# Storing two batches' last 64 tokens by one transfer, and the second batch's late Z behind the first relu, in the finish of an attention and spectral-mix kernel

## The chip, the cores and the metric

The kernel runs on one core of one Trainium2 chip. The metric is the time of one execution on the device, in microseconds (us). Engines are named as the profile names them: PE is TensorE (PEld its weight loads), DVE is VectorE, ACT is ScalarE, POOL is GpSimd, SP is SyncE, which issues all loads and stores here.

## The reference

Eight batches of 576 tokens go through attention with 8 heads of 64 and then through a spectral mix over the tokens. Cut to what matters:

```python
# attention: causal window of 128, a bias that falls with distance, softmax, then attn @ v
x = attn_out.transpose(0, 2, 1, 3).reshape(B, S, H * D)      # 8 x 576 x 512
X = np.fft.rfft(x, axis=1)[:, :64]                            # 64 modes of each batch
Yr = Xr @ w_r - Xi @ w_i ; Yi = Xr @ w_i + Xi @ w_r           # a 512 x 512 pair per mode
y = np.fft.irfft(Y, n=S, axis=1)
u = x + y
out = u + np.maximum(u @ w_ch, 0.0)                           # 8 x 576 x 512, float32
```

The two weight tensors of the modes are 64 x 512 x 512 float32 each and are read once: most of the traffic.

## The kernel before

**Stages.** Attention runs over pairs of heads and batches, its results stay in SBUF as `x_sb` and `x4`. The mode weights stream in through a ring (`_load_w`), and each mode's matmuls (`_modes`) follow. While the last weights stream in, the products `x @ w_ch` are made for all tiles (`_xw`, kept as `hl`). After the last weight comes `_finish` (L753 to L809), and only there does the output leave the core.

**Tiles.** The output is written in 36 tiles of 128 rows by 512 columns, listed in `g.seq` (L88 to L92). A batch has 576 = 4 x 128 + 64 tokens. So a pair of batches gives four full tiles of the first, four of the second, and one tile, `x4`, whose upper 64 rows are the last 64 tokens of the first batch and whose lower 64 rows are those of the second. The tiles are numbered 0 to 35; the mixed ones are 8, 17, 26 and 35.

**The finish.** The spectrum of a batch (`Z`, and `ZW = Z @ w_ch`) is complete for the first modes early. The last modes' part, the late Z, comes from `_z_late` (L710) into PSUM for four batches at a time, and `_z_take` (L730) copies one batch's 32 partitions of it to SBUF: `ZW` on ACT, `Z` on DVE, or on ACT for every fourth batch. Then the loop of L776 walks over the tiles:

- at step i PE makes tile i: `mm` is the argument of the relu and `y` the inverse transform, both in PSUM (`_known`, and the two `_pair` calls);
- then, at fixed steps, `_z_late` for batches 4 to 7 (L785) and `_z_take` for the batch whose first tile is three tiles ahead (L787);
- then tile i - 1 gets its nonlinearity. Tiles with way "a" take a relu on ACT (L794); tiles with way "q" take a copy of `y` on ACT (L797) and a maximum on DVE (L798). Tiles 0, 1 and the last five are "a", and two of each five between;
- then tile i - 2 gets its sum `o`, on DVE for "a" (L803) and on POOL for "q" (L806). `o` has 12 buffers (L801); `mm` and `y` have three PSUM buffers each, and a new tile takes the one that was freed first;
- `store` (L769) is called right behind the sum for "a", one step later for "q".

The order of the work on each engine is the order of these lines: it is written by hand, nothing moves it afterwards. SP takes the stores one after the other; each has one of eight completion semaphores in turn, so a store is issued only when the one eight before it has landed.

**The stores.** A tile that lies in one batch is stored as one transfer of 256 KB (L772). A mixed tile is stored as two transfers of 64 rows, 128 KB each (L774), since its halves lie 576 x 512 elements apart in the output.

Of the kernel before, what the change touches and what calls it, by code (L numbers as in the profile page):

```python
# [16 lines left out]
P = 128  # L17
# [16 lines left out]
def kernel(  # L34
# [60 lines left out]
    with tc.manual_schedule(engines={ET.SP, ET.PE, ET.Activation, ET.DVE, ET.Pool}):  # L95
        with ExitStack() as wctx:
# [116 lines left out]
            for m0, mg in todo:  # L213
                _modes(g, last, m0, mg, last=True)
                if NM - 4 <= m0 < NM - 1:
                    _idle(g, BUSY)
            mctx.close()
        _finish(g)


# [443 lines left out]
def _pair(nc, out, lhsT, rhs, **kw):  # L664

    for h in range(2):
        nc.tensor.matmul(  # L667
            out[64 * h : 64 * h + 64], lhsT=lhsT[h], rhs=rhs[h], tile_position=(0, 64 * h), **kw)
# [41 lines left out]
def _z_late(g, b0, psum):  # L710

    nc = g.nc
    zwp = psum.tile([P, g.DM], FP32, tag="zwp", name="zwl")
    zp = psum.tile([P, 4, P], FP32, tag="zp", name="zl")
    for et in range(4):
        for c in range(4):
            l = g.ZT[:, et, 3].rearrange("p a m b -> p (a m) b")[:, :, b0 + c]
            nc.tensor.matmul(
                zwp[32 * c : 32 * c + 32], lhsT=l, rhs=g.wch[:, et],
                start=(et == 0), stop=(et == 3), tile_position=(0, 32 * c))  # L720
    for et in range(4):
        for c in range(4):
            l = g.ZT[:, et, 3].rearrange("p a m b -> p (a m) b")[:, :, b0 + c]
            nc.tensor.matmul(
                zp[32 * c : 32 * c + 32, et], lhsT=l, rhs=g.ident_b, start=True, stop=True,
                tile_position=(0, 32 * c))
    g.late = (zp.rearrange("p a b -> p (a b)"), zwp)


def _z_take(g, b):  # L730
    nc = g.nc
    zp, zwp = g.late
    ks = slice(32 * (b % 4), 32 * (b % 4) + 32)
    nc.scalar.copy(g.ZW[ks, b], zwp[ks])
    if b % 4 == 2:
        nc.scalar.copy(g.Z[ks, b], zp[ks])
    else:
        nc.vector.tensor_copy(g.Z[ks, b], zp[ks])


def _known(g, i):

    nc = g.nc
    x = g.seq[i][0]
    g.mm[i] = g.fps.tile([P, g.DM], FP32, tag="mm", name="mm")
    g.y[i] = g.fps.tile([P, g.DM], FP32, tag="y", name="y")
    _pair(nc, g.mm[i], [g.ident2] * 2, [g.hl[:, i, h] for h in range(2)], start=True, stop=False)
    if g.way[i] == "a":
        _pair(nc, g.y[i], [g.ident_b[:, 0:64], g.ident_b[:, 64:128]], [x] * 2,
              start=True, stop=False)  # L750


def _finish(g):  # L753

    nc, tc = g.nc, g.tc
    N = len(g.seq)
    with ExitStack() as fctx:
        pool = fctx.enter_context(tc.tile_pool(name="fin", bufs=4))  # L760
        lps = fctx.enter_context(
            tc.tile_pool(name="lps", bufs=1, space=bass.MemoryType.PSUM, side="right"))
        first = [min(i for i, t in enumerate(g.seq) if t[1][0][0] == b and t[1][1][0] == b)
                 for b in range(g.B)]
        _z_late(g, 0, lps)
        _z_take(g, 0)
        o, r, y = {}, {}, {}

        def store(i):  # L769
            for h, (b, s) in enumerate(g.seq[i][1]):  # L770
                if h == 0 and g.seq[i][1][1] == (b, s + 64):
                    nc.sync.dma_start(out=g.out[b, s : s + P, :], in_=o[i])  # L772
                    break
                nc.sync.dma_start(out=g.out[b, s : s + 64, :], in_=o[i][64 * h : 64 * h + 64])  # L774

        for i in range(N + 3):  # L776
            if i < N:
                if i >= 3:
                    _known(g, i)
                ft = [g.FT[:, b % 4, s : s + 64] for b, s in g.seq[i][1]]  # L780
                _pair(nc, g.mm[i], ft, [g.ZW[:, b] for b, _ in g.seq[i][1]],
                      start=False, stop=True)
                _pair(nc, g.y[i], ft, [g.Z[:, b] for b, _ in g.seq[i][1]],
                      start=(g.way[i] == "q"), stop=True)
            if i == first[3] - 1:  # L785
                _z_late(g, 4, lps)
            for b in range(1, g.B):  # L787
                if i == first[b] - 3:
                    _z_take(g, b)
            j = i - 1  # L790
            if 0 <= j < N:
                r[j] = pool.tile([P, g.DM], FP32, tag="r", name="r")
                if g.way[j] == "a":
                    nc.scalar.activation(r[j], g.mm[j], AF.Relu)  # L794
                else:
                    y[j] = pool.tile([P, g.DM], FP32, tag="y", name="ys")
                    nc.scalar.copy(y[j], g.y[j])  # L797
                    nc.vector.tensor_tensor(out=r[j], in0=g.mm[j], in1=g.seq[j][0], op=ALU.max)  # L798
            j = i - 2
            if 0 <= j < N:  # L800
                o[j] = pool.tile([P, g.DM], FP32, tag="o", bufs=12, name="o")  # L801
                if g.way[j] == "a":
                    nc.vector.tensor_tensor(out=o[j], in0=g.y[j], in1=r[j], op=ALU.add)  # L803
                    store(j)
                else:
                    nc.gpsimd.tensor_tensor(out=o[j], in0=r[j], in1=y[j], op=ALU.add)  # L806
            j = i - 3
            if 0 <= j < N and g.way[j] == "q":
                store(j)  # L809
# [30 lines left out]
```

## Time and profile before

| What | Value |
|---|---|
| median of 3 runs | 446.2 us (445.45 to 446.92) |
| the profiled execution | 446.81 us, its span 445.0 us |
| busy share of the span: PE, DVE, ACT, POOL | 74%, 49%, 47%, 23% |
| DMA in the chain that ended last | 50% of the span |
| HBM read, written | 163.58 MB, 9.44 MB |
| stores of 256 KB | 32, median 3.0 us from issue to landing |
| stores of 128 KB | 8, median 2.7 us from issue to landing |
| last mode's sum on DVE ends, first store issued | 408.2 us, 412.0 us |

The span runs from the first to the last instruction of the profiled execution; the rest of its time lies outside. Line numbers are those of the kernel. In a row of the timeline the columns are the start, the length of the merged run, the engine, the line, the operation with its output and input, the shape and how many instructions were merged; the bracket names the idle time ahead of it and what ended it. "SPq" rows are DMA issues: their length is the issue on SP, not the transfer.

### The profile page before, as it was taken

Reading aid. Unit: us, or ns where it says so; the run is one execution under the profiler, and the core shown is the slowest. Engines: PE = TensorE matmul, PEld = TensorE weight load, DVE = VectorE, ACT = ScalarE, POOL = GpSimd, SP = SyncE. Lnnn points to the kernel's source line nnn. Section 1 sums busy time; section 2 is a strip of 40 time slices with the busy share of each in tenths; the row PEclk is TensorE's granted clock in tenths of the full one; section 3 lists DMA queues with packets and bytes.
Section 4 is the critical chain, followed back from the end, with each engine's and each line's share of the span. In section 5 each row is a group of like instructions: output and inputs, shape, how many; then the busy total and the mean of one; then the engine's idle time right before and its main releaser. Section 6 shows DMA issues by size and latency. Waiting matters only on the chain.

```text
span 445.0 us, 11009 instructions
## 1 busy us (share of the span) xinstructions
PE 327.6 (74%) x4626; PEld 217.1 (49%) x4654; DVE 219.2 (49%) x396; ACT 207.1 (47%) x313; POOL 101.6 (23%) x151
## 2 busy tenths in 40 slices
PE   2778889889979977467764656656665488869995
PEld 1445666666757654334443333333333355535553
DVE  6467867788758733242232323333233334512885
ACT  4799968999979501121322212212122132311884
POOL 8644535555533102000000000000000000000883
PEclk9999988999989855685566556566556669969999
DMA  8999989999999999999999999999999999992688
GB/s 294 395 389 385 404 321 399 392 404 405 406 406 402 406 409 404 417 423 425 422 423 425 419 415 418 426 423 423 424 423 423 425 410 417 416 422 122 252 313 288
DMA packets 55217, 173.73 MB, mean 390 GB/s; under 512 B 4992, under 2 KB 4992, under 8 KB 55168
## 3 DMA queue, kind: packets, MB, share of 16 engines
q1 hardware_dynamic: 55168, 173.04, 97.7%
q8 instruction: 36, 0.59, 0.5%
q14 instruction: 13, 0.11, 0.1%
HBM read 163.58 MB, written 9.44 MB: 389 GB/s over the span
## 4 chain that ended last, share of the span: by engine, by line
DMA 50%; PE 26%; ACT 12%; DVE 8%; issue 3%; SPq 1%; POOL 0%; ACTq 0%; POOLq 0%
DMA wi<-in_moe_w_i_dram 50%; PE acc L634 7%; ACT att L437 5%; ACT T L382 4%; DVE att L445 3%; PE mm L667 2%; PE idle L612 2%; PE tqk L372 2%; PE sc L431 2%; PE y L667 2%; PE xw L680 2%; PE av L462 1%; PE av L401 1%; DVE x_sb L480 1%; PE tp L658 1%
## 5 line engine op out<-in xcount | busy, mean ns | idle before, releaser
L684 ACT CAST hl<-xw 64x512 bf16<-64x512 f32 x72 | 41.8, 580 | 163.6 <-PE xw L680 126.1
L634 PEld LDWEIGHTS <-wi 128*128 128x128 bf16 x1024 | 65.7, 105 | 73.6 <-DMA wi<-in_moe_w_i_dram 71.7
L685 DVE TENSOR_TENSOR hl<-xw,hl 64x512 bf16<-64x512 f32 x72 | 49.6, 689 | 85.5 <-ACT hl L684 85.4
L634 PE MATMUL acc<-Xlast,wi 128*128 128x16 bf16 x768 | 55.9, 194 | 48.6 <-DMA wi<-in_moe_w_i_dram 48.5
L634 PEld LDWEIGHTS <-wr 128*128 128x128 bf16 x1024 | 70.7, 106 | 37.2 <-DMA wr<-in_moe_w_r_dram 26.4
L806 POOL TENSOR_TENSOR o<-r,ys 128x512 f32<-128x512 f32 x18 | 22.5, 1279 | 243.7 <-DVE r L798 242.3
L634 PE MATMUL acc<-Xlast,wr 128*128 128x16 bf16 x768 | 63.2, 194 | 19.4 <-DMA wr<-in_moe_w_r_dram 13.5
L445 DVE TENSOR_TENSOR att<-att,mask 128x1024 bf16<-128x1024 bf16 x64 | 55.9, 873 | 36.9 <-ACT att L437 36.6
L437 ACT ACTIVATE att<-sc 128x1024 bf16<-128x1024 f32 x64 | 66.7, 1043 | 9.9 <-PE sc L431 8.7
L382 ACT COPY T<-tqk 128x640 bf16<-128x640 bf16 x92 | 65.6, 767 | 1.7 <-PE tqk L372 1.7
L680 PE MATMUL xw<-wch,xT 128*128 128x512 bf16 x122 | 54.7, 577 | 4.9 <-issue 3.1
L372 PE MATMUL tqk<-ident_b,b 128*128 128x128 bf16 x432 | 39.4, 233 | 10.6 <-POOL b L362 6.4
L660 DVE COPY xT<-tp 128x512 bf16<-128x512 bf16 x36 | 15.2, 423 | 51.8 <-PE tp L658 50.8
L372 PEld LDWEIGHTS <-b 128*128 128x128 bf16 x432 | 27.3, 104 | 22.2 <-issue 11.0
L362 POOL CAST b<-v 128x576 bf16<-128x576 f32 x32 | 27.0, 871 | 17.6 <-issue 8.5
L680 PEld LDWEIGHTS <-xT 128*128 128x128 bf16 x144 | 19.0, 138 | 23.5 <-issue 21.6
L431 PE MATMUL sc<-T,T 64*128 64x256 bf16 (+2 forms) x320 | 26.9, 266 | 1.7 <-ACT att L437 1.0
L362 POOL CAST b<-q 128x576 bf16<-128x576 f32 x32 | 21.5, 699 | 28.9 <-issue 28.9
L362 POOL CAST b<-k 128x576 bf16<-128x576 f32 x32 | 22.0, 714 | 16.3 <-issue 8.5
L462 PE MATMUL av<-vn,att 128*128 128x65 bf16 (+1 forms) x576 | 25.3, 204 | 0.4 <-DVE vn L405 0.2
L462 PEld LDWEIGHTS <-att 128*128 128x128 bf16 (+1 forms) x576 | 21.3, 106 | 3.5 <-issue 0.2
L480 DVE TENSOR_TENSOR x_sb<-av,rec 128x512 bf16<-128x512 f32 x32 | 22.1, 692 | 1.1
(102 smaller groups left out, 437.8 us busy)
## 6 DMA issues: line engine op xcount, KB each, us to landing
wr<-in_moe_w_r_dram SPq DMA_DIRECT2D x85, 768.0 KB, 8.3
wi<-in_moe_w_i_dram SPq DMA_DIRECT2D x85, 768.0 KB, 9.7
q<-in_q_dram SPq DMA_DIRECT2D x32, 288.0 KB, 7.5
k<-in_k_dram SPq DMA_DIRECT2D x32, 288.0 KB, 6.1
v<-in_v_dram SPq DMA_DIRECT2D x32, 288.0 KB, 7.0
out_dram<-o SPq DMA_DIRECT2D x32, 256.0 KB, 3.0
wchf<-in_moe_w_ch_dram SPq DMA_DIRECT2D x4, 256.0 KB, 10.7
out_dram<-o SPq DMA_DIRECT2D x8, 128.0 KB, 2.7
```

Of the source, the lines that this page charges most:

```text
L362: g.nc.gpsimd.tensor_copy(u.b[w][:, :, e], u.raw[w][e])
L372: g.nc.tensor.transpose(u.tp[:, r - r0], u.b[w][:, r].rearrange("p u d -> p (u d)"), g.ident_b)
L382: copy(u.T[w].rearrange("c h (p r) -> c (h p) r", r=g.R)[:, :, r0:r1], u.tp[:, 0 : r1 - r0].rearrange("c r p -> c p r"))
L431: nc.tensor.matmul(sc[:, e, c0 : c0 + nq], lhsT=kT[es, h, _start(kt) : _start(kt) + P], rhs=qT[es, h, kt * P : kt * P + nq], start=True, s ...
L437: nc.scalar.activation(a, sc, AF.Exp, scale=1.0 / math.sqrt(g.D))
L445: nc.vector.tensor_tensor(out=a, in0=a, in1=m, op=ALU.mult)
L462: nc.tensor.matmul(av[o, h, t * (D + 1) : (t + 1) * (D + 1)], lhsT=u.att[min(kt // 2, 1), h][:, f, c0 : c0 + m], rhs=vn[:, g.ST * h + kt, ...
L480: nc.vector.tensor_tensor(out=xo, in0=avv[:, :, 0:4, 0:D], in1=rec[:, :, 0:4].unsqueeze(-1).broadcast_to([P, 2, 4, D]), op=ALU.mult)
L634: nc.tensor.matmul(acc[:, et, :, m - c0, :], lhsT=(wr, wi)[k][:, a].bitcast(BF16)[:, 1::2][:, et * P : (et + 1) * P], rhs=X[:, a, 1 - k : ...
L680: nc.tensor.matmul(xw, lhsT=xT[:, dt], rhs=g.wch[:, dt], start=(dt == 0 and g.way[n] != "q"), stop=(dt == 3))
L684: nc.scalar.copy(g.hl[hi, n, h], xw[hi])
L685: nc.vector.tensor_tensor(out=g.hl[lo, n, h], in0=xw[hi], in1=g.hl[hi, n, h], op=ALU.subtract)
```

## The change

The mixed tiles (8, 17, 26 and 35) are now stored by one transfer each, from 128 partitions of the tile to two blocks of 64 rows in the output. The `_z_take` of the second batch moves in step 1 from ahead of tile 0's relu to behind it; those of the other batches stay where they were.

```diff
         def store(i):
-            for h, (b, s) in enumerate(g.seq[i][1]):
-                if h == 0 and g.seq[i][1][1] == (b, s + 64):
-                    nc.sync.dma_start(out=g.out[b, s : s + P, :], in_=o[i])
-                    break
-                nc.sync.dma_start(out=g.out[b, s : s + 64, :], in_=o[i][64 * h : 64 * h + 64])
+            (b, t), (c, _) = g.seq[i][1]
+            rows = g.out[b, t : t + P, :] if b == c else g.out[b : c + 1, t : t + 64, :]
+            nc.sync.dma_start(out=rows, in_=o[i])
...
-            for b in range(1, g.B):
+            for b in range(2, g.B):
                 if i == first[b] - 3:
                     _z_take(g, b)
             j = i - 1
...
                     nc.vector.tensor_tensor(out=r[j], in0=g.mm[j], in1=g.seq[j][0], op=ALU.max)
+            if i == first[1] - 3:
+                _z_take(g, 1)
             j = i - 2
```

## The prediction

> **What bounds the kernel now.** I read the busy times by stage first. Columns: stretch and its length, PE, PEld, DVE, ACT and POOL busy with instruction counts, TensorE clock, DMA share, GB/s.
>
> ```profile
> 0.00:409.50 409.50, 298.61 (x4352) 200.01 (x4380) 191.97 (x354) 181.56 (x268) 79.04 (x133) 0.77 1.00 401
> 412.00:420.00 8.00, 7.85 (x78) 4.66 (x79) 7.50 (x13) 7.35 (x14) 6.99 (x6) 1.00 0.67 256
> 420.00:440.00 20.00, 19.13 (x190) 11.23 (x182) 17.03 (x27) 15.66 (x29) 15.55 (x13) 1.00 0.85 300
> 440.00:445.00 5.00, 0.00 (x0) 0.00 (x0) 0.69 (x1) 0.11 (x1) 0.00 (x0) 0.99 0.77 288
> ```
>
> Up to 409.5 us the loads fill all DMA engines (share 1.00); the change touches nothing there. In the finish TensorE is busy 98% and 96% of its two long stretches and paces 36 tiles at 0.8 us; the DMA engines have room (0.67, 0.85). The whole change lies in these last 35 us.
>
> The second view is SP's timeline, which holds the stores.
>
> ```profile
> 412.04 7.71 SPq L772 DMA_DIRECT2D out_dram<-o  x9
> 419.84 1.18 SPq L774 DMA_DIRECT2D out_dram<-o  x2
> 421.11 5.53 SPq L772 DMA_DIRECT2D out_dram<-o  x7
> 426.73 1.11 SPq L774 DMA_DIRECT2D out_dram<-o  x2
> 428.46 4.81 SPq L772 DMA_DIRECT2D out_dram<-o  x7
> 434.52 1.11 SPq L774 DMA_DIRECT2D out_dram<-o  x2
> 435.72 5.24 SPq L772 DMA_DIRECT2D out_dram<-o  x9
> 441.05 1.19 SPq L774 DMA_DIRECT2D out_dram<-o  x2
> ```
>
> Four pairs of half stores (L774) stand among 32 full ones; the last pair is the kernel's last work. The chain ends with what releases it:
>
> ```profile
> 439.51 0.61 ACT r L794
> 440.14 0.69 DVE o L803
> ```
>
> DVE ends at 440.83, SP issues at 441.05 and 441.64. The source view of L774 from 440.9 us gives 2.5 to 2.8 us to landing, so the last half lands at 441.64 + 2.5 = 444.14, and 0.86 us close the span of 445.0.
>
> How fast one DMA engine moves a row is in the stretches of half a microsecond at the end, where only stores move:
>
> ```profile
> 440.50:441.00 0.50, 0.00 (x0) 0.00 (x0) 0.34 (x1) 0.00 (x0) 0.00 (x0) 1.00 1.05 406
> 443.00:443.50 0.50, 0.00 (x0) 0.00 (x0) 0.00 (x0) 0.00 (x0) 0.00 (x0) 1.00 1.00 311
> ```
>
> All 16 engines are busy (share 1.0), also at 443, when little but the half stores is left: halves too are dealt to all 16. 406 GB/s over 16 is 25.4 GB/s for one engine, or 0.081 us for a row of 2,048 B. A full store puts 128/16 = 8 rows on each engine (0.65 us), a half 4.
>
> **The relu ahead of the second batch's Z.** Nothing is added; on ACT the second ZW copy and the first relu change places. DVE's order stays, since the first two tiles put no DVE instruction between the two places; PE's and POOL's stay; the step issues no DMA.
>
> ```profile
> 409.49 1.18 ACT L734 CAST ZW<-zwl 32x512 bf16<-32x512 f32 x2 [17.93 <-PE zwl L718]
> 410.69 1.09 ACT L794 ACTIVATE r<-mm 128x512 f32<-128x512 f32 x2
> 411.72 0.59 ACT L797 COPY ys<-y 128x512 f32<-128x512 f32 x1
> 412.50 0.59 ACT L797 COPY ys<-y 128x512 f32<-128x512 f32 x1 [0.20 <-PE y L667]
> 413.15 0.60 ACT L794 ACTIVATE r<-mm 128x512 f32<-128x512 f32 x1
> ```
>
> The first ZW copy ends at 410.07. The relu must wait for tile 0's mm on PE, which the timeline ends at 410.52, so it starts at most 0.17 us sooner than its 410.69, and ACT idles 0.45 to 0.6 us where the copy hid that wait. Behind it queue the copy (0.58), the second relu and tile 2's ys copy: the second relu goes from 411.18 to about 411.8, the ys copy ends near 412.9 instead of 412.31. PE's tile 4 waits for that, as its y takes the PSUM buffer the ys copy frees (starting at 412.49); tile 4's mm then goes from 413.11 to 413.6, and the relu at 413.15 follows. The 0.20 us of slack ahead of the copy at 412.50 is eaten. Against it, tile 0's add ends up to 0.17 sooner, and PE's 0.14 us pause ahead of tile 3's y (412.06 instead of 411.92) may go. Tile 4 itself reads the moved copy at 412.70; it is done by 411.9. I take +0.5 us on everything later, bounds -0.1 to +0.7, and PE has no later slack to absorb it.
>
> **The stores.** 40 issues become 36. A half costs SP 0.56 us (median of L774), but SP waits for its tiles most of the time (DVE's adds alone 13.0 us, its waits from 408 us), so in mid-finish fewer issues are worth 0. In the tail one full store issued at 441.05 with the 3.0 us to landing of the full stores around 440.4 lands at 444.05 instead of 444.14: 0.1 saved.
>
> But the new transfer is of a kind that the trace does not have. In the built program its source is 128 partitions of 2,048 B, its destination 2 x 64 rows with a stride between the two. Every transfer of before has one outermost count, 128 or 64, equal on both sides and a multiple of 16, and is dealt in equal parts of it. This one has 128 on one side and 2 on the other. The bounds are: still 16 parts of 8 rows (the full stores), or one part for each outermost item of the destination, two engines with 64 rows each. I take two parts: equal shares along the outermost count explain every row of the trace, while sixteen would need a cut inside the second dimension, which no transfer here shows. The DMA engines are then no longer interchangeable.
>
> The Trainium skill, page "DMA: Bandwidth & Descriptors", section "Why a DMA increments its semaphore by 16 and not by 1", states that a transfer uses the largest number of engines up to 16 that divides the slowest counts of both sides, and on this queue the lowest-numbered ones; by that the sum is the one below, with the same two engines each time. No run here shows it yet. The same page's "Rules for kernel authors" advises one 128-partition transfer in place of two halves, which speaks for the change and would give the 0.1 us above.
>
> Cost, if the same two engines serve all four merged stores: from the first of them on, each of the pair has 4 x 64 rows plus 8 rows of each of the 7 + 7 + 9 full stores behind, 440 rows, or 440 x 0.0807 = 35.5 us. Spread over 16 it was 216 rows. The window from 419.84 to 441 is 21 us, so the pair runs behind and never dries up: at 426.7 it holds about 5.2 + 4.5 - 5.9 = 3.8 us of work when the next 5.2 arrive. SP then waits for landings (a completion semaphore returns after eight stores), and through the 12 o buffers DVE, POOL and PE wait too; that delays issues, not the pair, which always has several stores queued. Around its rows a store needs 2.0 (fastest full store) - 0.65 = 1.35 us. End: 419.84 + 0.5 + 1.35 + 35.5 + 0.86 = 458.05, against 445.0: **+13.0 us**. The profiled execution took 446.81 with its span of 445.0, so it would take 459.8; the median of the runs, 446.2, lies 0.6 under it, which gives **459.2 us**.
>
> Bounds of this case: a row in 0.077 us, by the page's fastest slice (426 GB/s), -1.6; the relu at -0.1, -0.6; work already queued at the first merged store (halves there land in 3.4 us, the fastest in 2.2), +1.2; two instruction loads on the pair (36 of them take 0.5% of 16 engines' span, 1 us each), +2.0. That is 457.0 to 462.4.
>
> **Rivals.** *Sixteen engines after all*: place, the transfer's split; price, +0.5 from the relu and -0.1 at the last store, 446.6 us, not slower by anything measurable; with its bounds (-0.1 to +0.7; at most one issue of 0.6 saved) 445.5 to 446.8. It decides from about five parts on: the pair stops being the bound when 4 x 128/k + 184 rows fit into the 23 us from 421.2 to 444, some 285 rows, so k above 5. For it: all stores of before use 16. Against: none of them had an outer count below 16.
>
> *Another pair each time*: two engines per merged store, but not the same, so that the backlog drains between. Then only the last one shows: 441.05 + 0.5 + 1.35 + 5.2 + 1.0 queued (3.0 to landing less 2.0) + 0.86 = 450.0, +5.0, 451.2 us. Nothing in the trace tells which engines a narrower transfer gets.
>
> That the stores stay two transfers is excluded: the built program has 36, four of them 2x64x512.
>
> **How the numbers follow.** Same pair 0.82, another pair 0.06, sixteen 0.12. The likeliest gives 459.2. Its own range, 457.0 to 462.4, leaves out the other two cases and the edges of its bounds, so I reach down to the second pair case: 450.5 to 462.5. Faster or slower counts from 0.3% (1.3 us), about what a measurement of this kernel can tell from no change. Both two-engine cases are slower, 0.88; sixteen gives "same" 0.10, and 0.02 for a faster end that its bounds do not reach.
>
> **What would show it.** After the change, the page should list all 36 stores as 256 KB with a longer median to landing, the merged ones 7 us or more; the finish should move about 200 GB/s with a DMA share near 0.5, falling to 2 of 16 engines (0.13) at the end; new waits on landings of out must stand at SP, DVE L803 or POOL L806. The relu step shows as 0.45 us or more idle on ACT at 410.1 and tile 4's y on PE near 413.0. It is wrong if merged stores land in about 3 us, or if the DMA share in the last 5 us is still 0.8.

## The result and the profile after

The changed kernel takes 460.41 us (median of 5 runs, 459.63 to 461.11) against 445.98 us before (5 runs): a ratio of 1.032, 95% interval 1.030 to 1.034, or 14.4 us more. The forecast was 459.2 us, in a range from 450.5 to 462.5. The profiled execution took 459.95 us, with a span of 458.2 us. One of the 23 executions of the kernel before that stand beside the first four experiments took 754.67 us; the ratios leave it out.

The first ZW copy of the finish starts at 408.22 us in this profile and at 409.49 us in the one of before: the weights came in 1.3 us earlier here. So times within the finish are compared from that copy on: 50.0 us to the end of the span, before 35.5 us, which is the whole difference of the medians.

Busy times by stage of the kernel after, columns as in the prediction:

```profile
412.00:420.00 8.00, 7.78 (x92) 4.76 (x88) 6.99 (x11) 6.85 (x13) 7.56 (x7) 1.00 0.69 263
420.00:430.00 10.00, 9.78 (x96) 5.57 (x90) 8.37 (x14) 7.86 (x15) 8.17 (x7) 1.00 0.71 222
430.00:440.00 10.00, 8.63 (x77) 5.03 (x73) 7.30 (x12) 7.11 (x13) 6.66 (x6) 1.00 0.75 246
440.00:453.00 13.00, 0.38 (x4) 0.00 (x0) 1.35 (x2) 0.60 (x1) 0.00 (x0) 0.63 0.51 182
453.00:458.20 5.20, 0.00 (x0) 0.00 (x0) 0.00 (x0) 0.00 (x0) 0.00 (x0) 0.50 0.09 36
```

The engines still work through the tiles at nearly the old pace; the last sum on DVE starts at 440.8, 32.6 us after the first ZW copy, where before it was 30.7. From there on 17 us pass in which only stores move, where before it was 4. The end of that, us by us:

```profile
449.00:450.00 1.00, 0.00 (x0) 0.00 (x0) 0.00 (x0) 0.00 (x0) 0.00 (x0) 0.50 0.13 51
450.00:451.00 1.00, 0.00 (x0) 0.00 (x0) 0.00 (x0) 0.00 (x0) 0.00 (x0) 0.50 0.13 49
...
455.00:456.00 1.00, 0.00 (x0) 0.00 (x0) 0.00 (x0) 0.00 (x0) 0.00 (x0) 0.50 0.14 53
456.00:457.00 1.00, 0.00 (x0) 0.00 (x0) 0.00 (x0) 0.00 (x0) 0.00 (x0) 0.50 0.09 33
```

A DMA share of 0.13 is 2 of 16, steadily for 7 us, and 51 GB/s is two engines at 25.5, one row of 2,048 B in 0.080 us each. That is the pair, alone at work while the other fourteen have nothing left. The completions in the trace say the same of a store that is itself dealt to sixteen: of the full store that SP issued at 446.23 us, fourteen parts landed between 448.06 and 448.21 us, the other two at 451.19 and 451.33. That fits two engines whose older rows come first.

How many engines took part can also be counted on the page. For each part of a transfer on SP's queue the trace has one packet of 4 bytes behind the part's rows; they are the packets "under 512 B", and before there are 4992 of them for 312 transfers, 16 for each. The page of before, then that of after, with its only line for the stores:

```profile
DMA packets 55217, 173.73 MB, mean 390 GB/s; under 512 B 4992, under 2 KB 4992, under 8 KB 55168
```

```profile
DMA packets 55097, 173.73 MB, mean 379 GB/s; under 512 B 4872, under 2 KB 4872, under 8 KB 55048
...
out_dram<-o SPq DMA_DIRECT2D x36, 256.0 KB, 7.0
```

Before, 40 stores with 16 parts each are 640 of these packets. After, 32 stores with 16 and four with 2 are 520. The difference is 120, as the page has it. All 36 stores are of 256 KB, and their median to landing went from 3.0 to 7.0 us.

Who waits now, from SP's and DVE's lists of waits since 408 us (total us, times, longest):

```profile
SPq L835 <- DMA out_dram<-o: 9.1, 1, 9.1
SPq L772 <- DMA out_dram<-o: 5.6, 4, 3.5
```

```profile
DVE o L803 <- DMA out_dram<-o: 1.9, 2, 1.3
```

SP waits for landings before it may issue, DVE for an output buffer, and at the end SP waits 9.1 us for the last store. Before, landings cost SP 1.7 us at the end, and DVE nothing.

The relu step, on ACT and for tile 4's y on PE:

```profile
409.42 0.60 ACT L792 ACTIVATE r<-mm 128x512 f32<-128x512 f32 x1 [0.62 <-PE mm L667]
410.04 0.58 ACT L734 CAST ZW<-zwl 32x512 bf16<-32x512 f32 x1
410.64 0.60 ACT L792 ACTIVATE r<-mm 128x512 f32<-128x512 f32 x1
411.13 1.07 ACT L795 COPY ys<-y 128x512 f32<-128x512 f32 x2
```

```profile
411.76 0.41 PE L667 MATMUL y<-x_sb,ident_b 128*64 128x512 bf16 x2
```

ACT idles 0.62 us ahead of the relu, for PE's mm. Tile 4's y starts 411.76 - 408.22 = 3.54 us after the first ZW copy; before it was 412.49 - 409.49 = 3.00.

### The profile page after: what moved, and what is told of

Same layout as the page of the kernel before. It is cut to its first block, busy times and chain, and to the rows that moved or that the text cites. A ratio compares the mean times of both kernels' runs of the same rounds, so it can differ in the third digit from the quotient of the medians.

```text
span 458.2 us, 11032 instructions
## 1 busy us (share of the span) xinstructions
PE 331.8 (72%) x4654; PEld 215.8 (47%) x4654; DVE 219.3 (48%) x396; ACT 207.0 (45%) x313; POOL 101.1 (22%) x151
## 4 chain that ended last, share of the span: by engine, by line
DMA 46%; PE 25%; ACT 12%; DVE 9%; issue 2%; SPq 1%; POOL 0%; POOLq 0%; DVEq 0%; ACTq 0%
DMA wi<-in_moe_w_i_dram 44%; PE acc L634 6%; ACT att L437 6%; ACT T L382 4%; DVE att L445 3%; PE sc L431 2%; PE tqk L372 2%; PE idle L612 2%; DMA out_dram<-o 2%; PE av L462 2%; DVE x_sb L480 2%; PE xw L680 1%; PE av L401 1%; PE mm L667 1%; PE tp L658 1%
## 5 line engine op out<-in xcount | busy, mean ns | idle before, releaser
L806 POOL TENSOR_TENSOR o<-r,ys 128x512 f32<-128x512 f32 x18 | 22.5, 1274 | 245.8 <-ACT ys L795 243.1
L680 PE MATMUL xw<-wch,xT 128*128 128x512 bf16 x144 | 61.5, 574 | 0.0
L634 PE MATMUL acc<-X,wi 128*128 128x16 bf16 x256 | 18.5, 193 | 5.9 <-DMA wi<-in_moe_w_i_dram 5.9
```

The costliest lines, as they stand in the source:

```text
L634: nc.tensor.matmul(acc[:, et, :, m - c0, :], lhsT=(wr, wi)[k][:, a].bitcast(BF16)[:, 1::2][:, et * P : (et + 1) * P], rhs=X[:, a, 1 - k : ...
L680: nc.tensor.matmul(xw, lhsT=xT[:, dt], rhs=g.wch[:, dt], start=(dt == 0 and g.way[n] != "q"), stop=(dt == 3))
```

## The experiments

Theory A is the forecast's: each merged store is dealt to two DMA engines, always the same, and their queue becomes the bound. Theory B blames the two-block address pattern itself, theory C the moved copy. All kernels keep the order of before for the relu unless said.

| Run | Mixed tiles | Median us, beside before | Ratio, 95% interval |
|---|---|---|---|
| stores only | all merged | 460.43, 446.4 | 1.033 (1.030 to 1.036) |
| relu only | halves | 446.72, 446.4 | 1.0005 (0.999 to 1.002) |
| 62 and 2 rows | each half in two | 461.4, 446.4 | 1.035 (1.033 to 1.038) |
| 48 and 16 rows | each half in two | 446.2, 446.4 | 1.0006 (0.999 to 1.002) |
| last only | one merged | 452.26, 445.84 | 1.014 (1.013 to 1.016) |
| first three | three merged | 456.47, 445.84 | 1.023 (1.022 to 1.025) |
| 57 and 7 rows | each half in two | 452.52, 445.84 | 1.015 (1.014 to 1.017) |
| POOL's queue | all merged | 458.32, 445.84 | 1.027 (1.024 to 1.030) |
| last by 62 and 2 | last one's halves in two | 452.48, 445.67 | 1.013 (1.010 to 1.016) |
| nine buffers | all merged | 459.88, 445.67 | 1.031 (1.028 to 1.034) |

**The two parts of the change.** The merged stores alone (the diff's first part) and the moved copy alone (the rest of it).

> The merged stores alone; the second batch's late Z stays ahead of the first relu. Theory A (each merged store is dealt to two DMA engines, the same two each time, and these two become the bound of the finish): all but the relu's 0.5 us of the 14.4 us stays, 459.9 us against 446.0. Theory B (the two-block address pattern is slow by itself, in its issue or in each of its rows, on all engines): the same 459.9, so this run does not tell A from B. Theory C (the moved copy upsets the pipeline and the stores only suffer from it): close to 446.

> The moved copy alone, mixed tiles stored by halves as before. A and B: +0.5 us from the start of the finish on, 446.5 us; ACT idles about 0.6 us ahead of the first relu, and tile 4's y starts on PE 3.5 us after the first ZW copy instead of 3.0. C: most of the 14 us, 455 or more.

The stores alone cost 14.0 us, the copy 0.3 us by medians, which its interval does not part from nothing. C falls. In the trace of the copy alone the forecast's shift is there all the same: its first ZW copy starts at 408.97, and

```profile
410.17 0.60 ACT L794 ACTIVATE r<-mm 128x512 f32<-128x512 f32 x1 [0.62 <-PE mm L667]
```

```profile
412.51 0.41 PE L667 MATMUL y<-x_sb,ident_b 128*64 128x512 bf16 x2
```

the relu waits 0.62 us and tile 4's y starts 3.54 us after the ZW copy, as in the full change. From that copy to the end of the span it is 36.1 us against 35.5.

**Few engines without the pattern.** Before, with each half cut in two plain transfers; the control has other sizes.

```diff
-                nc.sync.dma_start(out=g.out[b, s : s + 64, :], in_=o[i][64 * h : 64 * h + 64])
+                for x, z in ((0, 62), (62, 64)):      # the control: ((0, 48), (48, 64))
+                    nc.sync.dma_start(
+                        out=g.out[b, s + x : s + z, :], in_=o[i][64 * h + x : 64 * h + z])
```

> Before, but each half of a mixed tile is stored as 62 rows and 2 rows: four plain transfers without a two-block pattern in place of two. A, if the split follows the largest divisor up to 16 of the outermost count: 62 = 2 x 31 and 2 both go to two engines, 31 and 1 rows each, 64 rows on the pair for each mixed tile, just as in the merged store, so 459.9 us although no pattern is used, within 1 us. B: plain rows are fast, only the eight more issues show, 447 us.

> The control of the 62 and 2 rows: each half stored as 48 and 16 rows, as many issues, but both counts divide by 16 (3 rows and 1 row on each engine). A and B: only the issues show, two more of 0.55 us behind the last sum and little in mid-finish, 446.5 to 447.3 us. If instead the number of transfers were what costs, this would be as slow as the 62 and 2 rows.

As many issues, the same bytes, no two-block pattern in either, and 15 us between them. The first took 461.4 us, 1.5 above the expected 459.9 and so more than the 1 us allowed, and no run shows what the rest is; the second took 446.2, a little under its 446.5 to 447.3. The page lines of the 62 and 2 rows, then of the 48 and 16:

```profile
DMA packets 55121, 173.73 MB, mean 378 GB/s; under 512 B 4896, under 2 KB 4896, under 8 KB 55072
```

```profile
DMA packets 55345, 173.73 MB, mean 391 GB/s; under 512 B 5120, under 2 KB 5120, under 8 KB 55296
```

Against 4992 the first has 96 completions fewer: 16 short transfers with 2 parts are 32 where 8 halves had 128. The second has 128 more: 16 with 16 parts are 256. So B falls as the cause of the 14 us, since plain rows cost as much, and the number of transfers costs nothing that can be seen. What counts is into how many parts the outermost count divides.

**How far the divisor goes.** The same edit with 57 and 7 rows.

> Each half stored as 57 and 7 rows. A with the divisor rule: 57 = 3 x 19 goes to three engines, 7 to seven of which three are the same, so 2 x (19 + 1) = 40 rows on each of the three for a mixed tile instead of 64. 4 x 40 + 23 x 8 = 344 rows instead of 440, 7.7 us less than the merged stores: 452.7 us, up to 1 us more for the issues. If odd counts were split as evenly as they go (4 rows on most engines): 446.2 us, as with 48 and 16.

452.52 us, within 0.2 of the row count's answer. That closeness is in part luck: against its own before the run cost 6.7 us, where the row count gives 14.0 - 7.7 = 6.3. The page and the end of the finish:

```profile
DMA packets 55169, 173.73 MB, mean 385 GB/s; under 512 B 4944, under 2 KB 4944, under 8 KB 55120
```

```profile
446.00:447.00 1.00, 0.00 (x0) 0.00 (x0) 0.00 (x0) 0.00 (x0) 0.00 (x0) 0.50 0.19 74
447.00:448.00 1.00, 0.00 (x0) 0.00 (x0) 0.00 (x0) 0.00 (x0) 0.00 (x0) 0.50 0.20 78
```

48 completions fewer are 8 transfers with 3 parts and 8 with 7 in place of 8 with 16 (80 for 128), and a share of 0.19 is 3 of 16.

**Whether the queue piles up.** Only the last mixed tile merged, or only the first three.

```diff
             for h, (b, s) in enumerate(g.seq[i][1]):   # ahead of it:
+            (b, t), (c, _) = g.seq[i][1]
+            if b != c and i == N - 1:                  # the other: i < N - 1
+                nc.sync.dma_start(out=g.out[b : c + 1, t : t + 64, :], in_=o[i])
+                return
```

> Only the last mixed tile is merged, the other three are stored by halves. A: nothing piles up before; the last store alone puts 64 rows on the pair, 5.2 us where a full store takes 0.65, so 446.4 + 4.5, 450.9 us. If a slow pattern cost the same for each merged store and the costs simply added up, a quarter of 14 us: 450.0 us, so the next run is needed to part them.

> The other way round: tiles 8, 17 and 26 merged, the last one by halves. A: the pair has 3 x 64 + 23 x 8 + 8 = 384 rows from the first merged store on instead of 440, 56 x 0.081 = 4.5 us less than all four merged: 455.9 us, though the nearest merged store is issued over 4 us ahead of the last one. A theory in which a merged store only costs while it is on its way itself (another pair each time, or a slow pattern hidden beside the other engines): earlier ones have landed when the last tile is stored, 446.4 to 448 us.

With the first three merged and the last one in halves, the kernel takes 10.6 us more than before, though all three merged stores are issued well ahead of the end. So the work stays queued on the same pair, and "another pair each time" falls for SP's queue: it allowed 2 us. The rows alone gave 9.5 us; 1.1 us was missing in that sum. The last one alone costs 6.4 us instead of 4.5. Its trace shows where, us by us:

```profile
442.00:443.00 1.00, 0.00 (x0) 0.00 (x0) 0.00 (x0) 0.00 (x0) 0.00 (x0) 1.00 0.52 174
443.00:444.00 1.00, 0.00 (x0) 0.00 (x0) 0.00 (x0) 0.00 (x0) 0.00 (x0) 0.58 0.11 18
444.00:445.00 1.00, 0.00 (x0) 0.00 (x0) 0.00 (x0) 0.00 (x0) 0.00 (x0) 0.50 0.11 23
445.00:446.00 1.00, 0.00 (x0) 0.00 (x0) 0.00 (x0) 0.00 (x0) 0.00 (x0) 0.50 0.13 51
446.00:447.00 1.00, 0.00 (x0) 0.00 (x0) 0.00 (x0) 0.00 (x0) 0.00 (x0) 0.50 0.13 51
```

From 443 to 445 the pair is busy (share 0.11) but moves 18 and 23 GB/s; only then does it reach its 51. At 51 these 41 KB would have taken 0.8 us, so 1.2 of the 1.9 us above the row count are lost there.

**Whether that creeping start is the pattern's.** The same with plain transfers: only the last tile's halves cut into 62 and 2 rows.

> Only the last mixed tile is cut into 62 and 2 rows twice; the other three are stored by halves. As with only the last tile merged, the pair has 64 rows at the very end, but by plain transfers. That run took 6.4 us more than before instead of 4.5; the rows of its merged store crept for some 2 us before they ran at their usual pace. A, if the creeping belongs to many rows on few engines as such: 452.3 us again. If it belongs to the two-block transfer: 450.4 us, plus up to 1 us for two more issues.

452.48 us: it creeps as well, at 18 and 33 GB/s in the same two microseconds (and at 39 and 37 in the next two, before it reaches 51):

```profile
443.00:444.00 1.00, 0.00 (x0) 0.00 (x0) 0.00 (x0) 0.00 (x0) 0.00 (x0) 0.72 0.10 18
444.00:445.00 1.00, 0.00 (x0) 0.00 (x0) 0.00 (x0) 0.00 (x0) 0.00 (x0) 0.50 0.10 33
```

So the two blocks are not what makes it; many rows on few engines is what the two kernels have in common. Why the first rows are slow, no run shows.

**Whether waiting for buffers costs.** The stores alone, with `bufs=9` instead of 12 for `o`.

> The merged stores alone, with 9 output buffers in place of 12, so that DVE, POOL and PE are held up earlier and more by landings. A: the pair has work queued all the time whatever the buffers are, so the end does not move: 460.4 us within 1.3, as with 12. If the time were lost by the engines that wait for buffers: three tiles less of lead, 3 x 0.8 = 2.4 us more, 462.8 us.

459.88 us, no longer than with 12, although the engines wait more. DVE's and POOL's lines with nine buffers:

```profile
DVE o L801 <- DMA out_dram<-o: 7.3, 3, 3.6
```

```profile
POOL o L804 <- DMA out_dram<-o: 4.3, 1, 4.3
```

They lose 11.6 us to landings where DVE lost 2.1 with twelve buffers (1.9 in the kernel after), and the end does not move: these waits are a consequence of the pair's queue, not the cost.

**Another queue.** All four merged, issued by `nc.gpsimd.dma_start`, the full stores by SP as ever.

> All four mixed tiles merged, but these four transfers are issued by POOL, the other 32 by SP. A, if the pair is the same for a transfer of this queue: 460 us again. If its transfers get another pair each time, the backlog of 56 rows (4.5 us) drains between them, since a full store brings 0.65 us of work each 0.8 us, and only the last one shows: 450 to 452 us. B: 460 us.

458.32 us, between the answers, so neither half of the expectation holds as it stands: it is 12.5 us above its own before, where the stores alone cost 14.0. The page's row for this queue, and a stretch near the end:

```profile
q0 software_dynamic: 2112, 1.06, 0.9%
```

```profile
451.00:452.00 1.00, 0.00 (x0) 0.00 (x0) 0.00 (x0) 0.00 (x0) 0.00 (x0) 0.50 0.20 78
```

In the trace's packet records the 2,112 packets are 256 of 4,096 B, that is two rows each, 1,792 of 8 B and 64 of 4 B. A packet of two rows has a median of 0.159 us, so a row costs 0.080 us as on SP's queue, and the price of a row is not what differs. The 64 completions are 16 for each of the four transfers, so on this queue they do not tell the number of parts. If all four transfers had the same pair, and each engine one packet at a time, never more than two of the 4,096 B packets would be on their way at once. The records have three at once in short moments between 445.5 and 447.0 us, and from 451 to 452 us a share of 0.20 is three engines of 16. So not all four fell on one pair; but with 12.5 us lost the backlog did not drain between them either. Which engines each took, the trace does not tell, and how the two queues share an engine stays open.

## Why the prediction was right

**Two parts, the same two, was the step that decided, and it held.** The completions (120 fewer), the share of 0.13 at the end, and the runs with 62 and 57 rows show the division by the outermost count on SP's queue; the first three merged show that the pair stays the same there. The rule of the Trainium skill, page "DMA: Bandwidth & Descriptors", section "Why a DMA increments its semaphore by 16 and not by 1", the largest number up to 16 that divides the slowest counts of both sides, agrees with each of them: 2 for 2 and 128, 2 for 62, 3 for 57, 7 for 7, 16 for 48. That they are the lowest-numbered engines, as it says, no run here can show; that they are the same ones, the first three merged do. The rival with sixteen engines is out.

**440 rows at 0.0807 us, 35.5 us.** At the steady 51 GB/s, 0.080 us a row, they are 35.2 us. In the packet records at least two engines are busy at every moment from 420.4 us, when the first merged store's rows begin, to 456.6, and the last landing stands at 457.10. That is 36.7 us for the 35.2 us of rows, a slow start (below) and the last landing, so the pair can have been dry for very little of it.

**The relu, +0.5 us.** The first merged store was issued 419.08 - 408.22 = 10.86 us after the first ZW copy; the first half store of before came 10.35 after it. 0.5, by the steps named: the idle 0.62 us, the ys copy, tile 4's y.

**What was too small: the time around the rows.** The sum gave 13.0 us, measured are 14.4. I allowed the first merged store 1.35 + 5.2 = 6.5 us to land; it took 7.6 (419.08 to 426.68), 1.1 us that I had only as an upper bound, "work already queued". The stretches around its start, in the kernel after:

```profile
420.00:420.25 0.25, 0.25 (x10) 0.14 (x4) 0.02 (x1) 0.00 (x0) 0.25 (x1) 1.00 1.08 410
420.25:420.50 0.25, 0.25 (x6) 0.12 (x4) 0.00 (x0) 0.00 (x0) 0.25 (x1) 1.00 0.27 82
421.00:422.00 1.00, 1.00 (x12) 0.49 (x10) 1.00 (x2) 1.00 (x3) 0.38 (x2) 1.00 0.40 55
```

The rows ahead of it ran out between 420.25 and 420.5, and its own begin at 420.4, 1.3 us after its issue; the first store of before, on idle engines, had its first packet 0.85 us after its issue (412.04 to 412.89). So by my estimate 0.4 us of the 1.1 were queued work, and the other 0.7 belong to the creeping start. That start held up other engines too: a share of 0.40 is six engines, which at 25.5 GB/s each would move some 160 GB/s and not 55. Closing the span took 1.1 us after the last landing instead of 0.86. That makes 14.3.

**The 0.1 us at the tail** is lost in the 14. The advice of the Trainium skill's page "DMA: Bandwidth & Descriptors", section "Rules for kernel authors", to use one 128-partition transfer in place of two halves, does not hold here: where the halves go to two blocks, the measurement decides against it.

**What would show it** came out on most points: landings of merged stores 7.6 to 9.6 us, waits on landings at SP and DVE, 0.13 at the end. A wait at L806 on POOL, which I had named as a possibility, is not there; with nine buffers POOL has one, at the same sum (L804 there). The DMA share of about 0.5 over the finish was too low up to 440 us (0.69 to 0.75), since the other fourteen engines still had their full stores.

## What to carry to other kernels

Before two transfers are merged into one, look at the outermost count on both sides: on SP's queue the number of engines followed from what divides it, and 256 KB on two of them are 64 rows on each, as many as eight such transfers put on each of sixteen. A narrow transfer in the middle of a stream is not hidden by being early: it delays everything behind it on its engines, and what counts is the sum of rows on the busiest one up to the end. The count of small packets on the page tells the number of parts without any timing, for transfers that SP issues; the four that POOL issued had 16 each, though their rows went through few engines at a time.

## What the runs showed that I had not expected

Rows on few engines start slowly: 18 to 33 GB/s for about 2 us, where the pair's steady rate is 51, in both kernels in which the pair's rows stood alone at the end. The kernel of 62 and 2 rows has such a microsecond at its first cut tile too (share 0.12, 18 GB/s between 421 and 422 us). A transfer that POOL issues went out in packets of two rows, 0.159 us each, with 1,792 packets of 8 B beside them for four transfers. And eight stores cut into sixteen, with counts that divide by 16, cost nothing that 10 runs could show (1.0006, 0.999 to 1.002).
